# A decode layer on one core: the softmax's cross-partition steps taken in pairs, its negation moved from GpSimd to ScalarE, and a direct broadcast query projection

## The chip, the cores and the metric

One core of one Trainium2 chip runs the whole program. The metric is the device time of one execution in microseconds, as the median of several executions. All runs told here are listed as fast, and only such runs are compared. Ratios are the mean time of one kernel's fast runs over that of the other's of the same rounds, so they are not quite the ratio of the medians that are quoted beside them. Lower is better.

"The span" is the time from the first to the last instruction in the trace; the measured time of an execution lies about 2 us above its span (1.7 to 2.1).

## The reference

One token per batch entry, two entries. Layer norm, a query projection, attention of 32 heads over the last 2048 positions of a cache of 8192, an output projection, a residual, and a gated feed-forward part:

```python
q = (x @ wq).reshape(B, 1, 32, 192)
k, v = k_cache[:, :, -2048:, :], v_cache[:, :, -2048:, :]
scores = einsum("bhqd,bhkd->bhqk", q, k) * 192 ** -0.5
o = einsum("bhqk,bhkd->bhqd", softmax(scores), v)
h  = x + o.reshape(B, 1, 32 * 192) @ wo
h2 = h + (gelu(ln(h) @ w_gate) * (ln(h) @ w_up)) @ w_down
```

There are 64 independent items (32 heads, 2 entries). Each needs its own 768 KB of K and 768 KB of V, so all 64 read 100.7 of the kernel's 122.3 MB.

## The kernel before

Each item's 2048 keys lie as 128 partitions of 16 keys. VectorE computes the scores, 16 multiply-and-sum instructions (`ttr`) of 128x192 an item, so an item's scores are a 128x16 tile. The softmax then needs a maximum and a sum across partitions. GpSimd makes them with `partition_all_reduce`, and negates the maximum so that ScalarE can use it as the bias of the exponential:

```python
# GpSimd
def armax(m):
    W(g, sem_v_max, m + 1)                       # VectorE's maximum of the 16 columns
    ins = g.partition_all_reduce(mb_[:, m:m + 1], m1[:, m:m + 1], channels=128, reduce_op=RMAX)
    W(g, sem_g_chain, sem_g_chain.inc(ins))
    ins = g.tensor_scalar(out=nm[:, m:m + 1], in0=mb_[:, m:m + 1], scalar1=-1.0, ..., op0=ALU.mult)
    assert sem_g_nm.inc(ins) == m + 1            # lets the exponential go
def arsum(m):
    W(g, sem_a_exp, m + 1)
    ins = g.partition_all_reduce(zb[:, m:m + 1], rs[:, m:m + 1], channels=128, reduce_op=RADD)
    assert sem_g_z.inc(ins) == m + 1             # lets the reciprocal go
for n in range(NIT + 2):
    arsum(n - 2); armax(n - 1)                   # ... bounds cut

# VectorE, item n: the small steps of earlier items stand among the 16 score instructions
for t in range(T):
    ins = v.tensor_tensor_reduce(out=junk[...], in0=kring[...], in1=qb_ring[...], ...,
                                 accum_out=s_all[:, n, t:t + 1])
    if t == 0 and n >= 1: rmax(n - 1)
    if t == 1 and n >= 2: rcp(n - 2)             # waits for arsum(n - 2)
```

TensorE then multiplies the exponentials with V (P·V, 16 matmuls an item), and every four items their rows are transposed and go through the output projection. The query comes from TensorE too: ten one-row matmuls (`qproj`) for four items, an eviction by ScalarE, and a matmul that spreads the row over 128 partitions. One queue (SyncE) issues all loads in order, with five buffers each for K and V; each load waits until its buffer's last user is done.

Of the kernel before, what the change touches and what calls it, by code (L numbers as in the profile page):

```python
# [5 lines left out]
BF16 = mybir.dt.bfloat16  # L6
# [19 lines left out]
GELU_C = 0.7978845608028654  # L26
# [7 lines left out]
NPIECE = 16  # L34
# [3 lines left out]
NCH = 3  # L38

# [16 lines left out]
def bass_sequential_preLN__sliding_block_cached__geglu_ffn__decode_kernel(  # L56
# [12 lines left out]
    with ExitStack() as ctx:  # L69
# [27 lines left out]
        q_sb = sb([1, 2, 2, 384], BF16)  # L97
# [10 lines left out]
        ones_row = sb([1, 128], BF16)  # L108
        lib_scr = sb([128, 2], F32)
        burn_rhs = sb([128, 512], BF16)  # L110
        ident = sb([128, 128], BF16)
        xin = sb([128, D], BF16)
# [9 lines left out]
        xT_ext = sb([128, 5, 33], BF16)  # L122
# [19 lines left out]
        q_ps = [ps([128, 512], F32) for _ in range(2)]  # L142
# [15 lines left out]
        sem_v_mv = S("v_mv")  # L158
        sem_v_in = S("v_in")
        sem_v_pr = S("v_pr")  # L160
        sem_p_qb = S("p_qb")
        sem_a_qb = S("a_qb")
        sem_v_init = S("v_init")
# [4 lines left out]
        sem_a_exp = S("a_exp")  # L168
        sem_a_oev = S("a_oev")
        sem_a_qev = S("a_qev")  # L170
        sem_a_otev = S("a_otev")
        sem_a_misc = S("a_misc")
        sem_a_chain = S("a_chain")
        sem_a_sd = S("a_sd")
        sem_a_gu = S("a_gu")
        sem_a_th = S("a_th")
        sem_a_ut = S("a_ut")
        sem_p_pv = S("p_pv")
        sem_p_q = S("p_q")
# [23 lines left out]

        QB_OFF = 256
# [10 lines left out]
        gbanks = [o_ps[0], o_ps[1], q_ps[0]]  # L215
        ubanks = [q_ps[1], h_ps_a, h_ps_b]
        dbank0 = o_ps[0]
        dbank1 = q_ps[1]

        @block.gpsimd  # L220
        def _(g):
            ins = g.iota(iota_i[:, :], pattern=[[-1, 128]], base=0, channel_multiplier=1)
            assert sem_g_misc.inc(ins) == 1
            W(g, sem_v_init, 1)
            ins = g.partition_all_reduce(lib_scr[:, 1:2], lib_scr[:, 0:1], channels=128, reduce_op=RMAX)
            assert sem_g_misc.inc(ins) == 2

            def armax(m):
                W(g, sem_v_max, m + 1)
                ins = g.partition_all_reduce(mb_[:, m:m + 1], m1[:, m:m + 1], channels=128, reduce_op=RMAX)  # L230
                W(g, sem_g_chain, sem_g_chain.inc(ins))
                ins = g.tensor_scalar(out=nm[:, m:m + 1], in0=mb_[:, m:m + 1], scalar1=-1.0, scalar2=None, op0=ALU.mult)  # L232
                assert sem_g_nm.inc(ins) == m + 1

            def arsum(m):
                W(g, sem_a_exp, m + 1)
                ins = g.partition_all_reduce(zb[:, m:m + 1], rs[:, m:m + 1], channels=128, reduce_op=RADD)  # L237
                assert sem_g_z.inc(ins) == m + 1

            for n in range(NIT + 2):  # L240
                if 0 <= n - 2 < NIT:
                    arsum(n - 2)
                if 0 <= n - 1 < NIT:
                    armax(n - 1)

        @block.sync
        def _(sp):
            sem_x.inc(sp.dma_start(xin[0:1, :], A_x[0, 0:1, :]), 16)
            sem_x.inc(sp.dma_start(xin[R1:R1 + 1, :], A_x[1, 0:1, :]), 16)
            for c in range(5):  # L250
                semWQ[0].inc(sp.dma_start(wqring[:, 0, c, :], wq_src(0, c)), 16)
# [6 lines left out]
            def mk_wq(J, c):  # L258
                def fn():
                    if J >= WQR and c == 0:  # L260
                        W(sp, sem_p_q, 2 * (J - WQR) + 2)
                    semWQ[J % WQR].inc(sp.dma_start(wqring[:, J % WQR, c, :], wq_src(J, c)), 16)
                return fn
# [16 lines left out]
            def mk_ffn(kind, c):  # L280
                def fn():
                    if kind == "g":
                        sem_wg.inc(sp.dma_start(wg_sb[:, c, :], B_w_gate[128 * c:128 * (c + 1), :]), 16)
                    else:
                        sem_wu.inc(sp.dma_start(wu_sb[:, c, :], B_w_up[128 * c:128 * (c + 1), :]), 16)
                return fn

            for c in range(5):
                add_aux(43 + 4 * c, mk_ffn("g", c))
                add_aux(45 + 4 * c, mk_ffn("u", c))  # L290

            for n in range(NIT):
# [5 lines left out]
                if n >= VS:  # L298
                    W(sp, sem_p_pv, n - VS + 1)
                semV[n % VS].inc(sp.dma_start(vring[:, n % VS, :], kv_src(A_v_cache, n)), 16)  # L300
# [4 lines left out]
            sem_out.inc(sp.dma_start(out[0, 0:1, :], h2_bf[0:1, :]), 16)  # L305
            sem_out.inc(sp.dma_start(out[1, 0:1, :], h2_bf[R1:R1 + 1, :]), 16)
            sp.wait_ge(sem_out.sem, 32)

        @block.vector
        def _(v):  # L310
# [17 lines left out]
            v.memset(eps_t[:, :], EPS)  # L328
            v.memset(ones_row[:, :], 1.0)
            assert sem_v_init.inc(v.memset(xT_ext[:, :, :].rearrange("p a b -> p (a b)"), 0.0)) == 1  # L330
            v.memset(burn_rhs[:, :], 0.0)
            W(v, sem_g_misc, 1)
            assert sem_v_init.inc(v.tensor_scalar(out=ident[:, :], in0=iota_i[:, :], scalar1=0.0, scalar2=None,  # L333
                                                  op0=ALU.is_equal)) == 2
            W(v, sem_x, 32)
            W(v, sem_v_init, 1)
            v.tensor_copy(x33f[0:1, :], xin[0:1, :])
            chain(v.tensor_copy(x33f[R1:R1 + 1, :], xin[R1:R1 + 1, :]))
            layernorm(x33f, stats, mv, sd1, rstd, xn_bf, 1, 1)
            v.memset(o_sb[0:33, :, :].rearrange("p a b -> p (a b)"), 0.0)  # L340
            v.memset(ot_flat[:, :], 0)
            v.memset(e_flat[:, :], 0)
            v.memset(hT_ext[:, :, :].rearrange("p a b -> p (a b)"), 0.0)
            assert sem_v_init.inc(v.memset(uT_flat[:, :], 0)) == 3

            def rmax(m):
                W(v, sem_v_ttr, m + 1)
                ins = v.tensor_reduce(out=m1[:, m:m + 1], in_=s_all[:, m, :], axis=AX.X, op=ALU.max)  # L348
                assert sem_v_max.inc(ins) == m + 1

            def rcp(m):
                W(v, sem_g_z, m + 1)
                ins = v.reciprocal(rinv[:, m:m + 1], zb[:, m:m + 1])  # L353
                assert sem_v_rcp.inc(ins) == m + 1

            def ttr(n):
# [6 lines left out]
                for t in range(T):  # L363
# [3 lines left out]
                    if t == 0 and n >= 1:  # L367
                        rmax(n - 1)
                    if t == 1 and n >= 2:
                        rcp(n - 2)  # L370
# [4 lines left out]
            rmax(NIT - 1)  # L375
            rcp(NIT - 2)
            rcp(NIT - 1)
# [6 lines left out]
            layernorm(h_sb, stats2, mv2, sd2, rstd2, hn_bf, 3, 2)  # L384
            for i in range(NCH):
                cs = slice(512 * i, 512 * (i + 1))
                W(v, sem_p_gu, i + 1)
                v.tensor_copy(u_bf[0:33, cs], ubanks[i][0:33, :])  # L388
                W(v, sem_a_gu, i + 1)
# [5 lines left out]
                W(v, sem_v_in, i + 1)  # L395
                chain(v.scalar_tensor_tensor(out=fA[0:33, cs], in0=g_bf[0:33, cs], scalar=0.5, in1=u_bf[0:33, cs],  # L396
                                             op0=ALU.mult, op1=ALU.mult))
                W(v, sem_a_th, i + 1)
                assert sem_v_pr.inc(v.scalar_tensor_tensor(out=fC[0:33, cs], in0=fB[0:33, cs], scalar=1.0,  # L399
                                                           in1=fA[0:33, cs], op0=ALU.add, op1=ALU.mult)) == i + 1  # L400
# [6 lines left out]
        def _(a):  # L407
            def achain(ins):
# [3 lines left out]
            a.activation(out=dum[0:1, 4:5], in_=dum[0:1, 5:6], func=ACT.Sqrt, bias=eps_t[0:1, :], scale=1.0)  # L412
            W(a, sem_v_mv, 1)
# [3 lines left out]
            ins = a.activation(out=xT_ext[:, :, 0:33:32], in_=t_ps[0][:, 0:10].rearrange("p (c b) -> p c b", b=2),  # L417
                               func=ACT.Copy)
            assert sem_a_misc.inc(ins) == 1

            def qev(j):
                W(a, sem_p_q, j + 1)
                if j >= 2:
                    W(a, sem_p_qb, 4 * j - 4)
                for b in range(2):
                    ins = a.activation(out=q_sb[0:1, j % 2, b, :], in_=q_ps[b][0:1, 0:384], func=ACT.Copy, scale=SCALE)  # L426
                    assert sem_a_qev.inc(ins) == 2 * j + 1 + b

            def qbev(m):
                W(a, sem_p_qb, m + 1)  # L430
                if m >= QBR:
                    W(a, sem_v_ttr, m - QBR + 1)
                ins = a.activation(out=qb_ring[:, m % QBR, :], in_=qb_bank(m)[:, QB_OFF:QB_OFF + DH], func=ACT.Copy)  # L433
                assert sem_a_qb.inc(ins) == m + 1

            def expo(m):
                h, b = m // 2, m % 2
                W(a, sem_g_nm, m + 1)
                if m >= ER:
                    W(a, sem_p_pv, m - ER + 1)  # L440
                else:
                    W(a, sem_v_init, 3)
# [4 lines left out]
            def oev(m):  # L447
# [4 lines left out]
                W(a, sem_v_rcp, m + 1)  # L452
# [12 lines left out]
            qev(0)  # L465
            qbev(0)
            qev(1)
            for n in range(NIT + 12):
                if n % 4 == 1:
                    j = (n + 3) // 4  # L470
                    if 2 <= j < NPIECE:
                        qev(j)
                if n + 1 < NIT:
                    qbev(n + 1)
                if 0 <= n - 1 < NIT:
                    expo(n - 1)
                if 0 <= n - 2 < NIT:
                    oev(n - 2)
                if n >= 8 and n % 4 == 0:
                    gq = n // 4 - 2  # L480
                    if gq < NGROUP:
                        otev(gq)

# [4 lines left out]
            a.activation(out=dum[0:1, 2:3], in_=dum[0:1, 3:4], func=ACT.Tanh)  # L488
            W(a, sem_p_misc, 2)
            ins = a.activation(out=hT_ext[:, :, 0:33:32], in_=t_ps[0][:, 0:10].rearrange("p (c b) -> p c b", b=2),  # L490
                               func=ACT.Copy)
# [206 lines left out]
```

## Time and profile before

| | before |
|---|---|
| median, us | 1005.23 (1000.41 to 1011.56, 15 runs) |
| span, us | 1004.2 |
| busy VectorE / TensorE / ScalarE / GpSimd | 32% / 27% / 9% / 7% |
| DMA, mean | 122 GB/s |
| mean TensorE clock | 0.57 of full |

Read it as a kernel in which nothing is busy. Such a profile is read by its waits, and the prediction below does that with its lines: the table of waits, one round of GpSimd's timeline, the source views of GpSimd's three lines, a saturated stretch of the DMA, and VectorE's first item.

### The profile page before, as it was taken

What the parts mean: (1) busy time and instruction counts of PE and PEld (TensorE: products, weight loads), DVE (VectorE), ACT (ScalarE), POOL (GpSimd) and SP (SyncE); (2) the same over time, 40 slices, a digit from 0 to 9 for tenths busy, and PEclk for the clock granted to TensorE, in tenths of its full rate; (3) what the DMA queues carried; (4) which work ended last, traced back from release to release, by engine and by line L of the source; (5) the groups of instructions that cost most, each with busy time, mean ns of one, the idle gap of its engine ahead of it and who ended that gap; (6) DMA issues with size and microseconds to landing.
All of it is one profiled execution on the core that took longest, in us unless ns stands there. A gap on an engine that the chain in (4) does not pass through costs nothing.

```text
span 1004.2 us, 6662 instructions
## 1 busy us (share of the span) xinstructions
PE 275.3 (27%) x1494; PEld 173.9 (17%) x1494; DVE 319.8 (32%) x2223; ACT 93.7 (9%) x324; POOL 66.3 (7%) x198
## 2 busy tenths in 40 slices
PE   3122122313313232321322231331321332321227
PEld 1111111212102121211211121121210211110123
DVE  5232332232233133233323313323223323223305
ACT  2001000100101010010100001010010100100003
POOL 0000000000000000000000000000000000000000
PEclk9555555555555555555555555555655556555658
DMA  9433234243233324324323423424324323422000
GB/s 348 185 142 110 114 126 154 78 161 126 79 145 142 113 103 154 126 86 153 126 94 137 162 84 136 175 78 171 140 82 159 141 83 141 147 83 104 0 0 1
DMA packets 28415, 122.73 MB, mean 122 GB/s; under 512 B 3156, under 2 KB 8280, under 8 KB 28376
## 3 DMA queue, kind: packets, MB, share of 16 engines
q1 hardware_dynamic: 28376, 122.31, 32.8%
q8 instruction: 12, 0.20, 0.1%
q14 instruction: 27, 0.22, 0.1%
HBM read 122.29 MB, written 0.00 MB: 122 GB/s over the span
## 4 chain that ended last, share of the span: by engine, by line
issue 87%; POOL 7%; PE 2%; ACT 2%; DVE 1%; POOLq 1%; ACTq 0%; DVEq 0%
POOL sb L237 3%; POOL sb L230 2%; POOL sb L232 2%; ACT sb L443 1%; PE ps L528 1%; POOLq L69 1%; DVE sb L364 0%; POOLq L232 0%; PE ps L665 0%; DVE sb L388 0%; PE ps L550 0%; PE ps L608 0%; DVE sb L396 0%; DVE sb L399 0%; DVE sb L393 0%
## 5 line engine op out<-in xcount | busy, mean ns | idle before, releaser
L580 PE MATMUL ps<-sb 128*33 128x192 bf16 (+1 forms) x1024 | 174.8, 363 | 708.6 <-ACT sb L443 708.6
L364 DVE CUSTOM_DVE_ANT_0 sb<-sb 128x192 bf16<-128x192 bf16 x1024 | 293.8, 351 | 2.0 <-ACT sb L433 2.0
L580 PEld LDWEIGHTS ps<-sb 128*33 128x33 bf16 (+1 forms) x1024 | 131.6, 134 | 741.0 <-ACT sb L443 722.3
L353 DVE RECIPROCAL sb<-sb 128x1 f32<-128x1 f32 x64 | 10.5, 163 | 661.7 <-POOL sb L237 661.7
L443 ACT ACTIVATE sb<-sb 128x16 bf16<-128x16 f32 x64 | 23.2, 363 | 660.6 <-POOL sb L232 660.6
L364 DVE DVE_READ_ACCUMULATOR2_ANT sb<- 128x1 f32 x1024 | 83.0, 81 | 0.0
L237 POOL PARTITION_ALL_REDUCE sb<-sb x64 | 25.7, 402 | 381.5 <-issue 381.5
L232 POOL TENSOR_SCALAR sb<-sb 128x1 f32<-128x1 f32 x64 | 16.7, 260 | 509.8 <-issue 509.8
L433 ACT ACTIVATE sb<-ps 128x192 bf16<-128x192 f32 x64 | 21.2, 331 | 210.8 <-PE ps L566 210.8
L550 PE MATMUL ps<-sb 128*1 128x384 bf16 x160 | 38.2, 401 | 0.5 <-ACT sb L417 0.3
L230 POOL PARTITION_ALL_REDUCE sb<-sb x64 | 28.2, 440 | 3.0 <-DVE sb L348 3.0
L455 ACT ACTIVATE sb<-ps,sb 1x192 bf16<-1x192 f32 x64 | 26.0, 406 | 6.7 <-DVE sb L353 5.9
L608 PE MATMUL ps<-sb 128*33 128x512 bf16 x48 | 24.5, 578 | 0.3 <-ACT sb L461 0.3
L566 PE MATMUL ps<-sb 1*128 1x192 bf16 x64 | 19.5, 304 | 1.6 <-ACT sb L433 1.1
L550 PEld LDWEIGHTS ps<-sb 128*1 128x1 bf16 x160 | 14.8, 99 | 18.1 <-issue 11.9
L610 PE MATMUL ps<-sb 128*33 128x128 bf16 x48 | 13.9, 289 | 0.0
L426 ACT ACTIVATE sb<-ps 1x384 bf16<-1x384 f32 x32 | 13.4, 464 | 3.5 <-PE ps L550 3.5
L443 ACT ACTIVATION_READ_ACCUMULATOR sb<-sb 128x1 f32 x64 | 11.9, 186 | 0.0
L528 PE MATMUL ps<-sb 128*33 128x512 bf16 x26 | 9.1, 523 | 9.1 <-DVE sb L333 9.1
L348 DVE TENSOR_REDUCE sb<-sb 128x1 f32<-128x16 f32 x64 | 10.5, 163 | 0.0
L566 PEld LDWEIGHTS ps<-sb 1*128 1x128 bf16 x64 | 6.1, 96 | 22.6 <-issue 20.5
L608 PEld LDWEIGHTS ps<-sb 128*33 128x33 bf16 x48 | 6.3, 131 | 13.2 <-issue 12.6
(68 smaller groups left out, 72.5 us busy)
## 6 DMA issues: line engine op xcount, KB each, us to landing
sb<-in_A_k_cache_dram SPq DMA_DIRECT2D x64, 768.0 KB, 5.8
sb<-in_A_v_cache_dram SPq DMA_DIRECT2D x64, 768.0 KB, 4.2
sb<-in_A_wq_dram SPq DMA_DIRECT2D x40, 192.0 KB, 5.7
sb<-in_A_wo_dram SPq DMA_DIRECT2D x16, 480.0 KB, 6.5
sb<-in_B_w_gate_dram SPq DMA_DIRECT2D x5, 384.0 KB, 6.3
sb<-in_B_w_up_dram SPq DMA_DIRECT2D x5, 384.0 KB, 6.2
sb<-in_B_w_down_dram SPq DMA_DIRECT2D x3, 640.0 KB, 6.6
sb<-in_A_x_dram SPq DMA_DIRECT2D x2, 1.2 KB
```

Source lines behind the costliest of these rows:

```text
L230: ins = g.partition_all_reduce(mb_[:, m:m + 1], m1[:, m:m + 1], channels=128, reduce_op=RMAX)
L232: ins = g.tensor_scalar(out=nm[:, m:m + 1], in0=mb_[:, m:m + 1], scalar1=-1.0, scalar2=None, op0=ALU.mult)
L237: ins = g.partition_all_reduce(zb[:, m:m + 1], rs[:, m:m + 1], channels=128, reduce_op=RADD)
L364: ins = v.tensor_tensor_reduce(out=junk[:, n % 2, t, :], in0=kring[:, slot, t * DH:(t + 1) * DH], in1=qb_ring[:, n % QBR, :], scale=1.0, s ...
L433: ins = a.activation(out=qb_ring[:, m % QBR, :], in_=qb_bank(m)[:, QB_OFF:QB_OFF + DH], func=ACT.Copy)
L443: ins = a.activation(out=e_ring[:, m % ER, :, _row(b)], in_=s_all[:, m, :], func=ACT.Exp, bias=nm[:, m:m + 1], scale=1.0, accum_out=rs[:, ...
L455: ins = a.activation(out=o_sb[r:r + 1, G % 2, (h % 2) * DH:(h % 2 + 1) * DH], in_=o_ps[m % 2][r:r + 1, 0:DH], func=ACT.Copy, scale=rinv[r: ...
L528: ins = pe.matmul(bank[0:33, 0:512], lhsT=ident[:, 0:33], rhs=burn_rhs[:, :], start=True, stop=True)
L550: ins = pe.matmul(q_ps[b][0:1, 0:384], lhsT=xT_ext[:, c, r:r + 1], rhs=wqring[:, J % WQR, c, 384 * half:384 * (half + 1)], start=(c == 0), ...
L566: ins = pe.matmul(t_ps[bank][:, QB_OFF:QB_OFF + DH], lhsT=ones_row[0:1, :], rhs=q_sb[0:1, j % 2, b, (h % 2) * DH:(h % 2 + 1) * DH], start= ...
L580: ins = pe.matmul(o_ps[m % 2][0:M, 0:DH], lhsT=e_ring[:, m % ER, t, 0:M], rhs=vring[:, m % VS, t * DH:(t + 1) * DH], start=(t == 0), stop= ...
L608: pe.matmul(h_ps_a[0:33, :], lhsT=ot_ext[:, k, 0:33], rhs=woring[:, gq % WOR, kk, 0:512], start=first, stop=last)
```

## The change

The author wanted fewer GpSimd steps and shorter dependent chains. The diff is cut to its core; cuts are marked with `...`.

```diff
+        GROUPS = [[2 * P, 2 * P + 1] for P in range(NIT // 2 - 1)] + [[NIT - 2], [NIT - 1]]
...
-            def armax(m):
-                W(g, sem_v_max, m + 1)
-                ins = g.partition_all_reduce(mb_[:, m:m + 1], m1[:, m:m + 1], channels=128, reduce_op=RMAX)
-                W(g, sem_g_chain, sem_g_chain.inc(ins))
-                ins = g.tensor_scalar(out=nm[:, m:m + 1], in0=mb_[:, m:m + 1], scalar1=-1.0, scalar2=None, op0=ALU.mult)
-                assert sem_g_nm.inc(ins) == m + 1
+            def armaxG(gi):
+                grp = GROUPS[gi]
+                a0, k = grp[0], len(grp)
+                W(g, sem_v_max, gi + 1)
+                ins = g.partition_all_reduce(mb_[:, a0:a0 + k], m1[:, a0:a0 + k], channels=128, reduce_op=RMAX)
+                assert sem_g_nm.inc(ins) == gi + 1
... (sum, maximum and reciprocal likewise by groups)
             def expo(m):
-                W(a, sem_g_nm, m + 1)
+                if m == grp[0]:
+                    W(a, sem_g_nm, gi + 1)
+                    sem_a_neg.inc(a.activation(out=nm[:, a0:a0 + k], in_=mb_[:, a0:a0 + k], func=ACT.Copy, scale=-1.0))
+                    W(a, sem_a_neg, gi + 1)
... (qproj, its eviction and the broadcast matmul go; the normed input is spread once at the start)
+                for c in range(5):
+                    ins = pe.matmul(t_ps[bank][:, QB_OFF:QB_OFF + DH], lhsT=xbc[:, b, c, :],
+                                    rhs=wqring[:, J % WQR, c, hoff:hoff + DH], start=(c == 0), stop=(c == 4))
... (the DMA queue)
-                semV[n % VS].inc(sp.dma_start(vring[:, n % VS, :], kv_src(A_v_cache, n)), 16)
+                if n >= 1:
+                    issue_v(n - 1)
+            issue_v(NIT - 1)
+            for c in range(5):
+                sem_wg.inc(sp.dma_start(wg_sb[:, c, :], B_w_gate[128 * c:128 * (c + 1), :]), 16)
+                sem_wu.inc(sp.dma_start(wu_sb[:, c, :], B_w_up[128 * c:128 * (c + 1), :]), 16)
... (feed-forward: sigmoid in place of tanh, evictions of u on ScalarE; 8 warm-up matmuls instead of 12; two memsets moved from VectorE to GpSimd; one output DMA)
```

## The prediction

> **What bounds the kernel now.** I read the page first, then the table of waits, then GpSimd's part of the timeline, then its source lines, then a few stretches of the DMA. The page says that no engine is busy: VectorE 32%, TensorE 27%, the DMA at 122 GB/s, and that the last chain is 87% "issue". So the time is in waits, and the waits form a ring:
>
> ```profile
> engine line waited for: us in total, times, longest us
> PE ps L580 <- ACT sb L443: 708.6, 64, 13.5
> DVE sb L353 <- POOL sb L237: 661.7, 64, 14.7
> ACT sb L443 <- POOL sb L232: 660.6, 64, 14.1
> POOL sb L232 <- issue: 509.8, 64, 10.3
> POOL sb L237 <- issue: 381.5, 64, 6.4
> ```
>
> TensorE's P·V (L580) waits for the exponential, ScalarE's exponential (L443) waits for GpSimd's negation (L232), VectorE's reciprocal (L353) waits for GpSimd's sum (L237). GpSimd itself waits for nothing that the profile shows: 509.8 us before the negation and 381.5 us before the sum, 891 of 1004 us. One round of it:
>
> ```profile
> start us, us, engine line op out<-in xcount [idle before <-releaser]
> 424.68 0.40 POOL L237 PARTITION_ALL_REDUCE sb<-sb  x1 [6.08 <-issue]
> 425.00 0.44 POOL L230 PARTITION_ALL_REDUCE sb<-sb  x1
> 425.12 0.16 DVE L353 RECIPROCAL sb<-sb 128x1 f32<-128x1 f32 x1 [10.28 <-POOL sb L237]
> 433.21 0.26 POOL L232 TENSOR_SCALAR sb<-sb 128x1 f32<-128x1 f32 x1 [7.77 <-issue]
> 433.50 0.36 ACT L443 ACTIVATE sb<-sb 128x16 bf16<-128x16 f32 x1 [9.26 <-POOL sb L232]
> 439.30 0.40 POOL L237 PARTITION_ALL_REDUCE sb<-sb  x1 [5.83 <-issue]
> ```
>
> The two all-reduces start 0.32 us apart and the reciprocal follows the first at once: an all-reduce is done in about 0.4 us. The silence lies only where GpSimd goes from all-reduce to TENSOR_SCALAR (7.8 us) and back (5.8 us). The source views of L237, L232 and L230 tell what stands there:
>
> ```profile
> L237 POOLq MODIFY_POOL_CONFIG  x128: 5/7/7, 33.3 to 972.7; - x128
> L232 POOLq MODIFY_POOL_CONFIG  x128: 83/83/83, 22.5 to 964.5; - x128
> L230 POOL PARTITION_ALL_REDUCE sb<-sb x64: 373/441/443, 22.2 to 964.1; - x64
> ```
>
> L232 and L237 each carry two reconfigurations an iteration, L230, which follows another all-reduce, has none. The last of L232 starts at 964.5, when the last L230 (964.1 + 0.44) is done, so the all-reduce was over and the 7.7 us after it were reconfiguration. The kernel is bound by 128 swaps, 14.9 us an item ((978.62 - 38.98) / 63, from the first to the last sum).
>
> **What the Trainium skill says.** "GPSIMD Engine Reference", 2.1 Instruction dispatch: the first call to a freshly loaded GpSimd kernel costs about 6 us with no visible profile instruction (measured there after MODIFY_POOL_CONFIG). The trace agrees on the return to the all-reduce (381.5 / 64 = 6.0 us) and shows more on the way to TENSOR_SCALAR (509.8 / 64 = 8.0 us). "Perfetto Trace Analysis", GPSIMD Engine Instruction: GpSimd's spans are unreliable, use start-to-start spacing; hence the checks above through consumers. "DMA: Bandwidth & Descriptors", Where 436 GB/s comes from: a fabric ceiling of 435 GB/s, about 358 for a core whose neighbour streams too. This trace moved 410 (below). "TensorE: Matmul & The Clock Gate", Part 1: half clock unless busy for some 3.4 us; here 0.50 in the stretches between bursts, 1.00 in the opening.
>
> **The change, part by part.**
> (1) The negation leaves GpSimd for ScalarE, one ACTIVATE of 128x2 per pair. After the first all-reduce GpSimd runs nothing but all-reduces, so the 128 swaps of the loop go; what is left are the two at the start (8.2 us before iota, 10.0 before the first all-reduce), hidden behind loads.
> (2) Items go in pairs: 33 groups, so 66 all-reduces instead of 128, about 66 x 0.44 = 29 us, off the path.
> (3) The query projection is made directly as broadcast: five 128-row matmuls per item instead of ten per four items plus a broadcast. At half clock 16 matmuls of 192 columns took 2.68 us (433.95 to 436.63), 0.167 each, so 0.84 us an item instead of 1.79/4 + 0.17 = 0.62; ScalarE loses 32 evictions of 0.46.
> (4) The V load goes one item later in the queue, gate and up weights go behind all K/V. The bytes stay.
> (5) The FFN gets sigmoid for tanh and the u eviction goes to ScalarE; less warm-up (8 instead of 12 matmuls); one output DMA.
>
> Once the ring is open, the next limits are the DMA, seen in a stretch of the opening, and VectorE, seen in its timeline there:
>
> ```profile
> core 0: us, PE busy (x) PEld busy (x) DVE busy (x) ACT busy (x) POOL busy (x), PEclk, DMA share, GB/s
> 8.00:28.00 20.00, 8.81 (x40) 3.51 (x40) 15.19 (x83) 4.32 (x10) 0.98 (x3) 0.86 1.02 410
> ```
>
> ```profile
> start us, us, engine line op out<-in xcount [idle before <-releaser]
> 17.17 0.36 DVE L364 CUSTOM_DVE_ANT_0 sb<-sb 128x192 bf16<-128x192 bf16 x1 [2.02 <-ACT sb L433]
> ...
> 21.92 0.17 DVE L348 TENSOR_REDUCE sb<-sb 128x1 f32<-128x16 f32 x1
> ...
> 26.46 0.17 DVE L348 TENSOR_REDUCE sb<-sb 128x1 f32<-128x16 f32 x1
> ```
>
> VectorE: between those two maxima, with the DMA saturated, an item took 4.54 us: 16 score ops of 0.278 (start to start, 17.17 to 21.92 for 17) and 0.09 for the maximum. Per pair after: 32 x 0.278 = 8.90, one maximum and one reciprocal of 0.09 to 0.1 each: 9.09. For 64 items 32 x 9.09 = 291 us.
> DMA: 3.15 MB of K/V a pair, and 15.7 MB of wq and wo over 32 pairs = 0.49 MB: 3.64 MB, at 410 GB/s 8.87 us. All 122.3 MB take 298 us. So VectorE and DMA are level, VectorE ahead by 2%.
> TensorE at half clock: 2 x (2.68 + 0.84) + tr and output projection (0.25 + 1.6 over two pairs, 0.93) = 7.97 us of 9.09. ScalarE about 2.6.
>
> Sum: first score at about 15.6 us (now 17.17; four warm-up matmuls less, but more broadcast copies), 291 us of scores, then the tail. In the old trace the last eviction at 979.31 to the end took 24.9 us; the FFN's three chunks (3.15 us each, 989.50 to 992.69) lose a 0.68 us cast from VectorE and swap two 0.68 us ops for 0.42, some 2 us in all. From the last score to that eviction: maximum 0.35, all-reduce 0.5, negation 0.25, exponential 0.45, P·V 2.7, latencies: 4.4. So 15.6 + 291 + 4.4 + 22.8 = 334, plus the 1 us by which the measured times exceed the span: 335. The FFN weights: issued after V of item 63, which leaves about 14 us before the last score; 5.9 MB take 14.4 us and are used 12 us after it: hidden.
>
> I add for what won't be perfect. The pair is a loop: first score of pair p+1, maximum of pair p (0.55), all-reduce (0.45), negation and exponential (0.75), two P·V (5.35), next query (0.98) and its eviction (0.36): 8.4 to 8.5 us, 0.6 under the 9.09 of VectorE. In every second pair the output projection (1.6 us) stands ahead of the second query, whose eviction stands ahead of the exponential on ScalarE: 9.3, so 0.2 us lost 16 times, 3 us. For stalls where VectorE meets a late K, 5 us. **342 us, a ratio of 0.34.**
>
> **Rivals.** (a) *The all-reduce is itself slow*, 6 to 8 us, and its record too short. Then 33 groups of about 14 us stay on GpSimd: 470 + 45 = 515 us. Against: the reciprocal right after 0.40 us, no gap between two all-reduces, the reconfiguration starting at its end. 3%.
> (b) *The query loop binds*: TensorE stays at half clock and the pair takes 9.6 to 10 us instead of 9.09: 335 + 32 x 0.7 = 357. For: only 0.6 us of slack, and a dozen waits in it. Against: bursts of over 5 us should raise the clock and shorten two P·V to half. 25%.
> (c) *The DMA binds*: the queue issues in order, V of an item waits for P·V in pairs, so the queue may run dry; at 360 GB/s sustained, 340 us of transfers + 4 + about 16 from the last weights = 360. For: 97% of the rate is needed. Against: five buffers of each are a lead of 4 items, 18 us. 20%.
> (d) *Score ops and all-reduces disturb one another*: at 22.19 an all-reduce ran 0.37 us among back-to-back score ops, so hardly. 5%.
>
> **Range and chances.** Everything perfect with a warm TensorE gives 330; (b) and (c) together some 370. 80% range 328 to 374. Only several unseen errors would leave it above 985: faster 0.98, same 0.01, slower 0.01.
>
> **What would show it.** Right if GpSimd shows MODIFY_POOL_CONFIG only at the start and no 6 to 8 us idle before L237's successor; VectorE's busy digits are 9 in nearly all slices and its wait for GpSimd gone; the DMA row is at 8 or 9 with 340 to 370 GB/s in the mean; the distance between pair maxima is about 9.1 us; and the last score lies some 27 us before the end. If that distance is over 9.5, the wait of the score ops tells whether the query's eviction (b) or a K transfer (c) is late. Idle before the all-reduce with the maxima 14 us apart would prove me wrong by (a). A TensorE clock still at 0.5 through the loop makes (b) likelier; a first score well after 16 us, or a tail over 30, misjudges only the ends.

## The result, and the profile after

| | before | after |
|---|---|---|
| median, us | 1005.23 | 334.27 (333.46 to 335.29, 8 runs) |
| ratio | 1 | 0.3326, 95% interval 0.3318 to 0.3334 |
| span, us | 1004.2 | 331.4 |
| busy VectorE / TensorE | 32% / 27% | 93% / 62% |
| DMA, mean | 122 GB/s | 370 GB/s |
| mean TensorE clock | 0.57 | 0.82 |

The page's slices, 8.3 us each, show a kernel whose VectorE hardly rests between its first and its last score (one stop, of 0.2 us), over a DMA that is at 90% or more until the tail:

```profile
DVE  1799999999999999999999999999999999999343
...
PEclk9955967878879775969897786977696898769999
DMA  6999999999999999999999999999999999969600
GB/s 227 408 416 414 410 412 413 415 409 413 412 410 413 403 411 392 391 418 384 414 381 402 397 413 404 407 404 404 410 376 407 349 408 353 380 262 407 254 2 0
```

The source views of GpSimd's lines show where reconfigurations are left. L243 (iota) and L248 (a first all-reduce whose result isn't used) have them, at 0.8 and 10.1 us, under the first loads. The all-reduces of the loop, L255 (maximum) and L262 (sum), have none:

```profile
L243 POOLq MODIFY_POOL_CONFIG  x2: 11/11/11, 0.8 to 0.8; - x2
L248 POOLq MODIFY_POOL_CONFIG  x2: 7/7/7, 10.1 to 10.2; - x2
L255 POOL PARTITION_ALL_REDUCE sb<-sb x33: 359/388/401, 25.6 to 307.5; - x33
L262 POOL PARTITION_ALL_REDUCE sb<-sb x33: 385/399/558, 28.4 to 308.7; - x33
```

In the table of waits GpSimd, which nobody seemed to hold up before, now waits for VectorE, and waits between the other engines are left that cost nothing, since the bound engine isn't among those that wait:

```profile
POOL sb L255 <- DVE sb L372: 226.1, 33, 7.3
ACT sb L458 <- PE ps L585: 147.0, 48, 5.8
PE ps L599 <- ACT sb L475: 100.1, 32, 7.8
ACT sb L469 <- POOL sb L255: 68.0, 32, 5.4
```

One pair in the timeline (start, duration, engine, line):

```profile
152.87 0.18 DVE L372 TENSOR_REDUCE sb<-sb 128x2 f32<-128x32 f32 x1
153.14 0.39 POOL L255 PARTITION_ALL_REDUCE sb<-sb  x1 [7.25 <-DVE sb L372]
153.56 0.20 ACT L469 ACTIVATE sb<-sb 128x2 f32<-128x2 f32 x1 [1.19 <-POOL sb L255]
153.80 0.36 ACT L475 ACTIVATE sb<-sb 128x16 bf16<-128x16 f32 x1
154.10 0.35 ACT L475 ACTIVATE sb<-sb 128x16 bf16<-128x16 f32 x1
154.25 2.91 PE L599 MATMUL ps<-sb 128*1 128x192 bf16 x32 [2.24 <-ACT sb L475]
154.58 0.40 POOL L262 PARTITION_ALL_REDUCE sb<-sb  x1 [1.05 <-ACT sb L475]
...
157.71 0.33 ACT L458 ACTIVATE sb<-ps 128x192 bf16<-128x192 f32 x1 [3.22 <-PE ps L585]
...
161.96 0.18 DVE L372 TENSOR_REDUCE sb<-sb 128x2 f32<-128x32 f32 x1
```

From the maximum of a pair to the exponential is now 0.93 us (152.87 to 153.80); before, GpSimd's part of that alone was over 8 us. The maxima of two pairs lie 9.09 us apart, and the query that the next pair needs is ready (157.71 + 0.33) almost 4 us before that next maximum.

The whole span divides as follows. The first score starts at 16.07 us, the last ends at 307.2, 291.1 us for 64 items. From there to the last row's eviction (310.15) it takes 2.9 us, and from there to the end 21.25 us.

### The profile page after: what moved, and what is told of

It reads as the page before. It is cut to its first block, busy times and chain, and to the rows that moved or that the text cites. A ratio compares the mean times of both kernels' runs of the same rounds, so it can differ in the third digit from the quotient of the medians.

```text
span 331.4 us, 6360 instructions
## 1 busy us (share of the span) xinstructions
PE 205.4 (62%) x1591; PEld 147.9 (45%) x1591; DVE 307.6 (93%) x2163; ACT 87.9 (27%) x331; POOL 28.7 (9%) x74
## 4 chain that ended last, share of the span: by engine, by line
DVE 72%; PE 18%; issue 5%; ACT 3%; POOL 1%; DVEq 0%; POOLq 0%
DVE sb L390 68%; PE ps L599 12%; PE ps L585 2%; DVE sb L372 1%; PE ps L664 1%; PE ps L553 1%; PE ps L667 1%; POOL sb L255 1%; ACT sb L475 1%; DVE sb L379 1%; ACT sb L458 1%; DVE sb L353 1%; ACT sb L469 0%; ACT L475 0%; ACT sb L527 0%
## 5 line engine op out<-in xcount | busy, mean ns | idle before, releaser
L599 PE MATMUL ps<-sb 128*33 128x192 bf16 (+1 forms) x1024 | 133.7, 306 | 102.1 <-ACT sb L475 100.1
L599 PEld LDWEIGHTS ps<-sb 128*33 128x33 bf16 (+1 forms) x1024 | 106.2, 112 | 128.5 <-ACT sb L475 109.8
L585 PE MATMUL ps<-sb 128*128 128x192 bf16 x320 | 38.6, 253 | 8.0 <-issue 3.9
L585 PEld LDWEIGHTS ps<-sb 128*128 128x128 bf16 x320 | 24.2, 99 | 19.9 <-issue 19.8
L255 POOL PARTITION_ALL_REDUCE sb<-sb x33 | 12.8, 387 | 226.1 <-DVE sb L372 226.1
L469 ACT ACTIVATE sb<-sb 128x2 f32<-128x2 f32 (+1 forms) x33 | 6.7, 203 | 68.0 <-POOL sb L255 68.0
L262 POOL PARTITION_ALL_REDUCE sb<-sb x33 | 13.5, 408 | 35.5 <-ACT sb L475 35.5
L629 PE MATMUL ps<-sb 128*33 128x512 bf16 x48 | 14.9, 383 | 0.5 <-ACT sb L493 0.5
L553 PE MATMUL ps<-sb 128*33 128x512 bf16 x22 | 6.4, 452 | 10.1 <-DVE sb L353 10.1
L631 PE MATMUL ps<-sb 128*33 128x128 bf16 x48 | 10.5, 219 | 0.0
L553 PEld LDWEIGHTS ps<-sb 128*33 128x33 bf16 x22 | 2.4, 114 | 13.3 <-DVE sb L353 10.1
L629 PEld LDWEIGHTS ps<-sb 128*33 128x33 bf16 x48 | 4.6, 96 | 6.7 <-issue 2.2
L379 DVE RECIPROCAL sb<-sb 128x2 f32<-128x2 f32 (+1 forms) x33 | 5.1, 156 | 1.6 <-POOL sb L262 1.6
L372 DVE TENSOR_REDUCE sb<-sb 128x2 f32<-128x32 f32 (+1 forms) x33 | 5.8, 176 | 0.0
L631 PEld LDWEIGHTS ps<-sb 128*33 128x33 bf16 x48 | 4.7, 98 | 0.0
```

The costliest lines, as they stand in the source:

```text
L255: ins = g.partition_all_reduce(mb_[:, a0:a0 + k], m1[:, a0:a0 + k], channels=128, reduce_op=RMAX)
L262: ins = g.partition_all_reduce(zb[:, a0:a0 + k], rs[:, a0:a0 + k], channels=128, reduce_op=RADD)
L372: ins = v.tensor_reduce(out=m1[:, a0:a0 + k], in_=s_all[:, a0:a0 + k, :], axis=AX.X, op=ALU.max)
L553: ins = pe.matmul(bank[0:33, 0:512], lhsT=ident[:, 0:33], rhs=burn_rhs[:, :], start=True, stop=True)
L585: ins = pe.matmul(t_ps[bank][:, QB_OFF:QB_OFF + DH], lhsT=xbc[:, b, c, :], rhs=wqring[:, J % WQR, c, hoff:hoff + DH], start=(c == 0), stop ...
L599: ins = pe.matmul(o_ps[m % 2][0:M, 0:DH], lhsT=e_ring[:, m % ER, t, 0:M], rhs=vring[:, m % VS, t * DH:(t + 1) * DH], start=(t == 0), stop= ...
```

## The experiments

Every kernel ran on a chip beside runs of the kernel before. Three things were to be told apart: which part of the change brought the gain, what limits the kernel now, and how much room the other parts have. Three of the kernels (experiments 6 to 8) computed something wrong on purpose and were still found correct within the tolerance, presumably because attention adds little to this output. So "correct" says little about the scores here.

### 1. The negation alone

The kernel before, with one thing changed:

```diff
                 ins = g.partition_all_reduce(mb_[:, m:m + 1], m1[:, m:m + 1], channels=128, reduce_op=RMAX)
-                W(g, sem_g_chain, sem_g_chain.inc(ins))
-                ins = g.tensor_scalar(out=nm[:, m:m + 1], in0=mb_[:, m:m + 1], scalar1=-1.0, scalar2=None, op0=ALU.mult)
                 assert sem_g_nm.inc(ins) == m + 1
...
                 W(a, sem_g_nm, m + 1)
+                achain(a.activation(out=nm[:, m:m + 1], in_=mb_[:, m:m + 1], func=ACT.Copy, scale=-1.0))
```

> The kernel before, with the negation alone moved from GpSimd to ScalarE; no pairs, no other part of the change. Theory (the 128 reconfigurations were the bound): all of them leave the loop, VectorE becomes the limit with 16 x 0.278 + a maximum and a reciprocal of 0.09 each = 4.63 us an item, 296 us for 64; with 17 us ahead and 31 us of tail 344 us, within 337 to 356. Rival 1 (the all-reduces are slow themselves): still about 14 us an item, over 900 us. Rival 2 (pairing does a good part of the gain): 500 to 700 us.

Measured: 344.3 us, ratio 0.3422 (0.340 to 0.3445). Of the 671 us between the two kernels (1005.2 - 334.3), this one line brings 661 us. VectorE's timeline has its maxima 4.60 us apart, against 4.63 expected:

```profile
202.06 0.16 DVE L346 TENSOR_REDUCE sb<-sb 128x1 f32<-128x16 f32 x1
...
206.66 0.16 DVE L346 TENSOR_REDUCE sb<-sb 128x1 f32<-128x16 f32 x1
```

### 2. A copy on GpSimd in place of the TENSOR_SCALAR

Experiment 1 takes away an instruction as well as the reconfigurations. This one keeps an instruction at the same place, on the same engine, with the same wait, and changes only its kind:

```diff
-                ins = g.tensor_scalar(out=nm[:, m:m + 1], in0=mb_[:, m:m + 1], scalar1=-1.0, scalar2=None, op0=ALU.mult)
+                ins = g.tensor_copy(nm[:, m:m + 1], mb_[:, m:m + 1])
```

> The kernel before, with GpSimd's TENSOR_SCALAR in the loop replaced by a plain copy on GpSimd (the exponential's bias becomes plus the maximum in place of minus; after the division by the sum the result is mathematically the same). It tells an elementwise instruction on GpSimd from the reconfiguration that TENSOR_SCALAR brought. Theory, if a copy needs no reconfiguration: none in the loop, some 0.3 us more a step on GpSimd, off the path, 340 to 360 us. If a copy needs one too: 1000 us and 128 pairs of reconfigurations. Rival 1 (any GpSimd elementwise step next to an all-reduce costs the 8 us): 1000 us without reconfigurations.

Measured: 347.27 us, ratio 0.345 (0.3437 to 0.3464). The source view of the line has the copy and no MODIFY_POOL_CONFIG (nor has that of the sum):

```profile
L232 POOL COPY sb<-sb x64: 183/388/392, 23.0 to 316.2; 128x1 f32<-128x1 f32 x64
```

So a copy on GpSimd, in place of ScalarE's negation, costs about 3 us in the whole run (347.3 against 344.3), and what cost 660 us was that this step was of a kind for which GpSimd was reconfigured, there and back. This is the experiment that settles the cause. (That the TENSOR_SCALAR is slow by itself would not explain the way back: the same all-reduce of the sum came 6.0 us late in the mean behind a reconfiguration in the kernel before, and here, without one, waits only for the exponential.)

### 3. The negation put back, by pairs

The changed kernel with GpSimd's TENSOR_SCALAR, once per pair, in place of ScalarE's copy:

```diff
                 ins = g.partition_all_reduce(mb_[:, a0:a0 + k], m1[:, a0:a0 + k], channels=128, reduce_op=RMAX)
+                W(g, sem_g_chain, sem_g_chain.inc(ins))
+                ins = g.tensor_scalar(out=nm[:, a0:a0 + k], in0=mb_[:, a0:a0 + k], scalar1=-1.0, ..., op0=ALU.mult)
...
-                    sem_a_neg.inc(a.activation(out=nm[:, a0:a0 + k], in_=mb_[:, a0:a0 + k], func=ACT.Copy, scale=-1.0))
-                    W(a, sem_a_neg, gi + 1)
```

> The changed kernel with the negation put back on GpSimd, by pairs. Theory: 33 groups with two swaps each, 8.0 + 6.0 us, plus two all-reduces, the negation and the exponential in between, 0.5 + 0.4 + 0.26 + 0.5, = 15.6 us a group: 33 x 15.6 = 515 us, less the overlap of the swaps with waits, plus 26 us ahead of the first group and 22 us of tail: 540 us, within 510 to 565. Rival (the reconfigurations overlap the other work when groups are larger): near 335 us.

Measured: 710.14 us, ratio 0.7048 (0.7011 to 0.7085). The direction is as the theory has it, the size is not: 170 us more than I worked out. One group in the timeline:

```profile
304.17 0.25 POOL L257 TENSOR_SCALAR sb<-sb 128x2 f32<-128x2 f32 x1 [8.45 <-issue]
...
310.32 0.41 POOL L265 PARTITION_ALL_REDUCE sb<-sb  x1 [5.89 <-issue]
310.76 0.17 DVE L382 RECIPROCAL sb<-sb 128x2 f32<-128x2 f32 x1 [10.79 <-POOL sb L265]
...
315.01 0.18 DVE L375 TENSOR_REDUCE sb<-sb 128x2 f32<-128x32 f32 x1
315.30 0.39 POOL L255 PARTITION_ALL_REDUCE sb<-sb  x1 [4.57 <-DVE sb L375]
...
325.50 0.25 POOL L257 TENSOR_SCALAR sb<-sb 128x2 f32<-128x2 f32 x1 [9.81 <-issue]
```

The group takes 21.3 us here (20.6 in the mean of the first 30). GpSimd is idle for 4.57 us before its maximum: VectorE stood at the reciprocal until the sum was done (10.79 us), and only after it could the 14 remaining score instructions of that item run and the next maximum be taken. I had summed GpSimd's own work and forgotten that a wait inside VectorE's program holds back everything behind it.

### 4. The same with the reciprocal later

```diff
-        RCP_AT = {grp[-1] + 2: gi for gi, grp in enumerate(GROUPS)}
+        RCP_AT = {grp[-1] + 3: gi for gi, grp in enumerate(GROUPS)}
```

> The run with the negation back on GpSimd by pairs took 710 us where I expected 540. Its trace has a group of 20.7 us: reconfiguration and negation 9.2, exponential 0.7, reconfiguration and sum 6.3, and 4.5 us in which GpSimd waits for the next maximum, because the reciprocal stands between the second and third score instruction of an item, and those behind it can't start before the sum. Here the reciprocal stands one item later, behind the next maximum. If that is the cause, the 4.5 us go and the query loop is what is left: 0.55 + 0.4 + 9.2 + 0.5 + two P.V 5.4 + 1.4 = 17.4 us, 31 x 17.4 + 26 + 30 = 595 us, within 570 to 620. Rival (the reconfigurations are longer in this kernel for another reason): 700 us.

Measured: 641.21 us, ratio 0.6365 (0.6341 to 0.639). The 69 us that it gained are half of what the 4.5 us a group would give (31 x 4.5 = 140), so the reason is right and not the whole of it; the time lies above my range. GpSimd's waits in this kernel show why: the idle time before the maximum fell from 143.8 us in experiment 3 to 27.1, but the reconfigurations ahead of the TENSOR_SCALAR grew (by 45 us in all). VectorE hardly waits at the reciprocal any more (37.7 us, against 379.2); it stands ahead of its scores instead (266.6 us), so the query loop is what is left, as expected. My sum was also short of rounds: it counted 31, but the two single groups at the end took 18.1 and 14.1 us as well.

```profile
POOL sb L257 <- issue: 338.2, 33, 11.5
POOL sb L265 <- issue: 195.9, 33, 6.4
POOL sb L255 <- DVE sb L375: 27.1, 26, 6.7
```

That is 10.2 us each, against 8.9 in experiment 3 (292.8 / 33) and 8.0 in the kernel before, while the way back stays at 6 us. The traces show with what the one way grows: the DMA. Worked out from the packets of each trace, the mean busy share of the DMA in these gaps was 34%, 38% and 59% in the kernel before, experiment 3 and experiment 4. Within each kernel the gaps go with it too: they took 7.1 to 7.2 us in the mean where the DMA was idle (two to four gaps in each of the three kernels), and 10.5 us in experiment 4 where its share was 50 to 70% (24 gaps). That the transfers slow the reconfiguration is likely, but no run here changes one of the two alone.

### 5. Groups of one

```diff
-        GROUPS = [[2 * P, 2 * P + 1] for P in range(NIT // 2 - 1)] + [[NIT - 2], [NIT - 1]]
+        GROUPS = [[m] for m in range(NIT)]
```

> The changed kernel with groups of one item instead of pairs: 64 all-reduces of each kind, 64 maxima, 64 reciprocals, all without reconfiguration. Theory (pairing is worth only its instructions on VectorE): 31 maxima and 31 reciprocals more at 0.09 us each, 5.6 us, so a ratio of 1.01 to 1.02 to the changed kernel, 336 to 342 us. Rival (pairing also makes the TensorE bursts long enough for the higher clock, without which the query loop is too slow): 350 us or more, with the TensorE clock near 0.5.

Measured: 337.91 us, ratio 0.3358 (0.3344 to 0.3371), 1.0% over the changed kernel. The TensorE clock is 0.873 in the mean, so short bursts don't take it down, and the rival falls. Pairing, which is the most visible part of the diff, is worth 3.6 us, VectorE's 31 maxima and 31 reciprocals (5.6 us by my sum).

### 6. Half of the score work

Every score instruction runs over 96 of its 192 columns:

```diff
-  out=junk[:, n % 2, t, :], in0=kring[:, slot, t * DH:(t + 1) * DH], in1=qb_ring[:, n % QBR, :],
+  out=junk[:, n % 2, t, 0:DH // 2], in0=kring[:, slot, t * DH:t * DH + DH // 2], in1=qb_ring[:, n % QBR, 0:DH // 2],
```

> The changed kernel with every score instruction over 96 of the 192 columns (wrong result on purpose). VectorE's item falls from 4.54 to about 2.9 us, the bytes stay. Theory (VectorE is the limit by 2%, the DMA right behind): the time falls only to what the DMA allows, 122.3 MB at 410 GB/s = 298 us plus about 4 us at the start and 12 to 18 us after the last bytes: 314 to 324 us, DMA row at 9 throughout. Rival (the loop over all-reduce, exponential, P.V and next query sets the pace at 9.09 us a pair): 331 to 335 us as before.

Measured: 328.38 us, ratio 0.326 (0.3255 to 0.3265). A third of VectorE's busy time is gone (307.6 to 210.2 us) and the time falls by 1.8% (2.0% by the ratios). VectorE's waits name the reason:

```profile
DVE sb L390 <- DMA sb<-in_A_k_cache_dram: 87.3, 57, 3.4
```

The theory holds; the time is 4 us above my range. The tail after the last bytes is not the reason: the last weights landed at 315.3 us, and 11 us were left, less than the 12 to 18 allowed. The bytes came later than the 302 us worked out, because the 410 GB/s did not hold to the end (the last slices of the page have 369, 272, 387 and 272 GB/s among them).

### 7. Half of V

```diff
-  semV[n % VS].inc(sp.dma_start(vring[:, n % VS, :], kv_src(A_v_cache, n)), 16)
+  semV[n % VS].inc(sp.dma_start(vring[:, n % VS, 0:T * DH // 2], kv_src(A_v_cache, n)[:, 0:T * DH // 2]), 16)
...
-  rhs=vring[:, m % VS, t * DH:(t + 1) * DH]
+  rhs=vring[:, m % VS, (t % 8) * DH:(t % 8 + 1) * DH]
```

> The changed kernel with half of each V transfer (each of the 8 row blocks loaded is used twice; wrong result on purpose): 25 MB less. Theory (VectorE limits): no change, 331 to 335 us, VectorE busy in all slices. Rival (DMA limits): 25 MB at 410 GB/s = 61 us less, 275 us.

Measured: 334.02 us, ratio 0.3316 (0.3311 to 0.3321): 25 MB less and no change. With experiment 6 this puts VectorE in front and the DMA about 2% behind it.

### 8. Both halves

> Both halves together (wrong result on purpose): VectorE 5.8 us and DMA 6.9 us a pair. Shows the next limit. If it is the DMA still: 97 MB at 410 GB/s = 237 us + 20 = 255 us. If it is the loop of maximum, all-reduce, negation, exponential, two P.V, query and eviction: with P.V between 1.4 and 2.7 us at full and half clock it is 5.6 to 8.4 us a pair, 16 + 32 x 5.6..8.4 + 24 = 220 to 310 us. My guess 265.

Measured: 271.04 us, ratio 0.2694 (0.2687 to 0.2701). The page still has the DMA at 9 in nearly every slice between the start and the tail, at 325 to 419 GB/s, and VectorE at 5 to 9; VectorE waits for K only 23.4 us. The 271 us lie over the 255 of a pure DMA bound, so several limits meet here, and I don't name one.

### 9. P·V twice

```diff
-                for t in range(T):
+                for t in list(range(T)) * 2:
```

> The changed kernel with the 16 matmuls of each P.V issued twice (the second pass starts the sum anew, so the result is right). It puts a load on the query loop that the prediction's rival (b) was about. Theory (longer bursts hold the TensorE clock up): P.V doubled takes 2.8 us, the loop is 0.55 + 0.45 + 0.75 + 5.6 + 0.6 + 0.36 = 8.3 us, under 9.09: 331 to 338 us, clock over 0.9. Rival (clock stays at half): P.V 5.35 each, loop 13.8 us, 470 us.

Measured: 344.0 us, ratio 0.3415 (0.3409 to 0.342), clock 0.945. The rival's 470 us is far off, but my range was too low by 6 us. Of the 10.8 us more of span (342.2 against 331.4), 1.4 are a later first score (17.47), 2.0 a longer tail with its doubled last P·V, and 7.1 are seven stops of VectorE in the loop. The first is of 2.9 us, after the first pair, whose P·V took 8.12; the other six are of 0.7 us. The lines below show one of the six: P·V, the query, its eviction, and the score that had to wait for it.

```profile
95.48 7.20 PE L599 MATMUL ps<-sb 128*1 128x192 bf16 x64 [1.98 <-ACT sb L475]
...
102.62 0.59 PE L585 MATMUL ps<-sb 128*128 128x192 bf16 x5
...
103.24 0.33 ACT L458 ACTIVATE sb<-ps 128x192 bf16<-128x192 f32 x1 [7.51 <-PE ps L585]
...
103.70 0.36 DVE L390 CUSTOM_DVE_ANT_0 sb<-sb 128x192 bf16<-128x192 bf16 x1 [0.71 <-issue]
```

In most pairs the 64 matmuls took 5.55 us at full clock. In this one the clock was down for a part, they took 7.20, the query came at 103.57, and VectorE stood for 0.71 us. That is the loop of the prediction's rival (b), caught where it binds: with P·V at 7.2 us a pair. In the changed kernel P·V of a pair takes 2.9 to 5.4 us.

### 10. The old order of the DMA queue

The changed kernel, with V of an item issued right behind its K and the gate and up weights among items 43 to 61, as before:

```diff
-                if n >= 1:
-                    issue_v(n - 1)
-            issue_v(NIT - 1)
-            for c in range(5): ...      # gate and up weights
+                issue_v(n)
... (gate and up weights as in the kernel before)
```

> The changed kernel with the old order of the DMA queue: V of an item right behind its K, gate and up weights in the middle of the run. Theory (queue order is hidden by five buffers of each): within 1%, 331 to 337 us, perhaps some us more, since K transfers behind a blocked V come later and 3.9 MB of weights stand ahead of K and V. Rival (the new order is needed for the DMA to keep up): 345 us or more with VectorE waiting for K.

Measured: 342.0 us, ratio 0.3395 (0.3389 to 0.3401), 2.1% over the changed kernel and outside my range. VectorE now waits for K:

```profile
DVE sb L397 <- DMA sb<-in_A_k_cache_dram: 5.8, 9, 1.8
```

All nine stops lie after 230 us, when weights had been put among the K and V transfers; further, the first score came 1.2 us later. With a reserve of 2%, the order of the queue is worth 7.7 us. The edit moves V and the weights together; where the stops lie points to the weights, but no run separates the two. I had called this part "the bytes stay" and given it nothing.

Pairs (3.6 us, experiment 5) and order (7.7 us), each taken out of the changed kernel, make 11.3 us, about the 10 us that lie between experiment 1 and the changed kernel. The direct query projection and the new feed-forward part were not tested alone.

### 11. Two or three of sixteen scores shared with ScalarE

Experiments 6 and 7 say that of VectorE's time and the bytes of V only VectorE's time is worth anything, and no more than about 2%. So of the 16 score instructions two (or three) become one VectorE multiply, whose products ScalarE sums, being 27% busy:

```diff
+                ins = v.tensor_tensor(out=mulp[:, n % 2, :] ..., in0=kring[:, slot, 0:RO * DH] ...,
+                                      in1=qb_ring[:, n % QBR, :] ... , op=ALU.mult)       # RO = 2 or 3
-                for t in range(T):
+                for t in range(RO, T):
...
+            def red(m):                                     # ScalarE, first in its item
+                for t in range(RO):
+                    ins = a.activation(out=rjunk[:, m % 2, t, :], in_=mulp[:, m % 2, t * DH:(t + 1) * DH],
+                                       func=ACT.Copy, accum_out=s_all[:, m, t:t + 1])
```

> A try at a faster version: of the 16 score instructions of an item, two are replaced by one VectorE multiply of 2 x 192 columns whose products ScalarE sums with an accumulating copy. Theory (VectorE at 4.545 us an item is the limit, and the DMA-bound time is the 328.4 us of the run with halved score work): VectorE's item falls by 0.556 us less the multiply, 0.27 to 0.47 us by how fast it runs, to 4.26 to 4.46 us: 328 to 332 us, a ratio of 0.985 to 0.995 to the changed kernel. Rival (the two sums on ScalarE, 0.3 us each, delay query eviction or exponential and lengthen the loop): 334 us or more.

> The same with three of the 16. VectorE's item 4.0 to 4.3 us, under the 4.43 us of the DMA: DMA-bound, 328 to 330 us; more cannot come of it. Rival as for two: ScalarE in the way, 334 us or more.

Measured: 328.93 us with two, ratio 0.3267 (0.3258 to 0.3277); 328.77 us with three, ratio 0.3258 (0.325 to 0.3266). Both beat the changed kernel by 1.8 and 2.0% (0.3267 / 0.3326, 0.3258 / 0.3326; 1.6% by the medians), and both reach the 328.4 us of experiment 6 and stop there: VectorE waits for K, 9.5 us with two and 10.6 with three. From the start of the multiply of 384 columns to the next score it took 0.271 us, against the 0.556 of the two instructions that it replaced (2 x 0.278, start to start as well). Its products are stored as bf16 before they are summed; whether that costs precision was not measured: as said, the check of correctness here is too mild to weigh that.

## Why the prediction was right

The time was 334.27 us, inside 328 to 374, and 2.3% under the 342 us named. Point by point:

- *The bound is the reconfiguration of GpSimd, not the all-reduce.* Right, and shown by experiments 1 and 2: 661 of the 671 us. Rival (a) would have left 515 us. Experiment 3 shows that halving the number of reconfigurations doesn't even halve the time, if they stay on the path.
- *VectorE, 9.09 us a pair, 291 us.* The trace has 9.09 and 291.1.
- *DMA level with it, 2% behind.* Experiments 6 and 7: 1.8 to 2.0%. So rival (c), the DMA as the bound, was wrong by little; VectorE never waited for K in the changed kernel.
- *First score at 15.6.* It was 16.07. One likely reason is in the trace, on the chain to that score: VectorE's conversion of the iota, of 0.23 us in the kernel before, took 1.67 (8.35 to 10.02) beside the memsets that GpSimd now runs (8.27 to 9.94).
- *Tail of 4.4 + 22.8 us.* It was 2.9 + 21.25; P·V of the last item ran at full clock and the feed-forward chunks came closer than I worked out. These two errors of the ends, +0.5 and -3.0, make the 334 of span 331.4. The measured time of an execution lies about 2 us above its span (1.7 to 2.1) and not 1, so the 335 worked out is hit within 1 us partly by luck: errors of both signs cancel.
- *The 8 us added for imperfection.* This is the term that was mis-sized, and the reason why 342 stands where 335 was worked out. Of it, 5 us were for late K: no K came late. 3 us were for the query loop with TensorE at half clock, in every second pair: the mean clock was 0.82, and VectorE's only stop in the loop, 0.20 us at 34.44, was one late query, of the first pair, where a table load of 1.28 us stood ahead of the exponential.
- *Part (3), the query on TensorE.* The comparison mixes two clocks: 0.84 us an item is worked out at half clock, but the 1.79 us of the old ten matmuls are those of the opening, at full clock (later, with the clock down, they took up to 3.16). With the clock down the old way comes to about 3.16/4 + 0.17 = 0.96 us (an estimate), so the direct projection costs TensorE no more. The sum rests on the 0.84 alone.
- *Part (4), "the bytes stay".* Wrong in its silence: the order of the queue is worth 2% (experiment 10). It didn't show because the change had the better order.
- *Part (2), the pairs.* Right as "off the path": 1.0% (experiment 5).
- *Rival (b).* Right to fear, wrong in size. The argument against it, that bursts of over 5 us raise the clock, held only in part: P·V of seven pairs took 5.4 us, and the clock over the first of these was 0.51. But the loop had room even so: in the other six the next query was ready 1.0 to 1.2 us before its score, where I had 0.6. It was seen to bind at 7.2 us of P·V a pair (experiment 9).
- *Rival (d).* Not seen: the score instructions beside an all-reduce kept their distance of 0.28 us.

What stays open: whether it is the DMA's traffic that stretches the reconfiguration ahead of a TENSOR_SCALAR from 7 to over 10 us, and which limit holds the run with both halves at 271 us.

## What to carry to other kernels

When a profile shows every engine idle, look for the engine that others wait for and that itself waits for "issue", and ask what its queue does there: here MODIFY_POOL_CONFIG stood in the queue with a duration of 0.01 to 0.08 us and the 6 to 8 us after it belonged to nobody. On GpSimd, keep inside a loop to instructions between which the trace shows no reconfiguration (here all-reduce and copy), and give the odd one to an engine with room. Once a bound falls, the next ones may lie within 2% of one another, so work out all of them, and mind in-order programs, in which one early wait (the reciprocal) holds back everything behind it.

## What the Trainium skill lacked or had wrong

- "GPSIMD Engine Reference", 2.1 Instruction dispatch, gives about 6 us for the first call to a freshly loaded kernel. The runs agree for the way back to the all-reduce (6.0 us in the kernel before, 6.0 and 5.9 in experiments 3 and 4). The way to TENSOR_SCALAR took more: 8.0 us in the mean before, 6.9 to 7.7 at its end when the DMA was quiet, 8.9 and 10.2 in experiments 3 and 4, where the DMA was busier. The page doesn't say that it is paid anew at every alternation, 128 times here.
- No page that I found says which GpSimd instructions can follow one another freely. The runs show: all-reduce and COPY in both directions, and MEMSET after IOTA, without a reconfiguration; all-reduce and TENSOR_SCALAR in both directions, and an all-reduce after IOTA (10.0 us in the kernel before) or MEMSET (10.9 us in the changed kernel), with one.
- "TensorE: Matmul & The Clock Gate", Part 1, tells when the clock is at half or full. Here one 64-matmul burst met both (7.20 us against 5.55), a burst of 5.4 us stayed at 0.51, and the mean of the run was about 0.8, which the page alone didn't let me foresee; I took half for the worst case and full for the best.
